# Attention output through DRAM in one transfer, heads laid out by halves of tokens, weight slices used two pieces behind the load

## The chip, the cores and the metric

One core of a Trainium2 chip runs the whole kernel. The metric is the device time of one execution in microseconds (us); the kernel before is given by the median of three runs.

## What is computed

Two blocks over 2048 tokens of width 512, each behind a layer norm whose shift, scale and gate come from a condition vector `c`: multi-query attention (32 heads of width 16, one shared key and value head), and a gated feed-forward part of width 1792 without a nonlinearity.

```python
mod = (_silu(c) @ w_mod).reshape(c.shape[0], 6, 1, -1)        # sa, ca, ga, sb, cb, gb
h = _layernorm(x) * (1 + ca) + sa
q = heads(h @ wq); k = h @ wk; v = h @ wv                     # 32 heads of q, one of k and v
p = softmax(einsum("bhqd,bkd->bhqk", q, k) * 16 ** -0.5)
x = x + ga * (heads_joined(einsum("bhqk,bkd->bhqd", p, v)) @ wo)
h = _layernorm(x) * (1 + cb) + sb
x = x + gb * (((h @ w_gate) * (h @ w_up)) @ w_down)
```

## The kernel before

**Units.** After a lead-in, the kernel runs 32 units, one for every 256 tokens (`ST`) and 128 columns of q (8 heads, one of four chunks `ch`). Within a unit, two heads stand side by side along the 512 columns of a matmul (`BT`): index `a` (0, 1) picks the half of the partitions, index `p` (0, 1) the plane of the tile `sst`, and `c` (0, 1) the half of the 512 columns. Before the change head 4p + 2c + a lies there, and `sst` is laid out as [p, (c, n)].

**Turns and steps.** A unit has 16 turns, one per 128 keys, and a turn has two steps, so 32 steps in a unit (`NSTEP`). In a turn TensorE computes scores of this unit (`qk_exp`, lines 645-657), ScalarE their exponential, TensorE adds probabilities times values of the turn before into one PSUM bank (`pv`, line 664), and TensorE with VectorE find the row maxima of the unit to come (`max_mm`, lines 590-608). Between them stand "side" matmuls (line 508): q projections, output projection and the feed-forward part of earlier tokens. The program order of every engine is written out by `attend` (line 1210) and nothing is reordered later; each engine runs its own list in order and waits only where data or a buffer is missing.

**The result of a unit.** `pv_out` (line 667) stands at the end of turn 1 of the next unit. ScalarE evicts the bank to `ev` (line 670). Ten transfers on the queue of SyncE (SP) follow: two put the sums of the softmax into DRAM (`rs`, line 675), eight lay the eight heads one below the other in the tile `oc` (line 681). `normalise` (line 683) has three parts, placed by `NORM_AT` at steps 5, 12 and 18: `load` brings the sums back spread over 128 partitions (line 688); `recip` inverts them on VectorE (line 691), writes them to DRAM (`ri`, line 693) and at once reads them back repeated for each head's 16 rows (`rr`, line 695); `mult` scales `oc` on GpSimd (POOL, line 700) and makes two halves in 16 bits.

**The side list.** `late_weights` (line 887) returns a list of items, each with a gap in steps to the next; `side_step` (line 1169) takes at most one per step. What an item issues comes at the start of the turn after its step (`posts`, drained at line 1242); the matmuls of the `sums` items are issued at their own step. Three kinds matter here.
- `norms` (line 957): 36 slices of `wo`, `w_gate` and `w_up` are loaded through SP (`stage`, line 925, load at line 931), and one item later squared and added up on POOL (`square`, lines 938 and 940). `sums` (line 942) adds these over the partitions on TensorE (line 950). Gaps: `SQ_GAP`, and `SUM_GAP` once.
- `pipelined` (line 1077): the same slices are loaded again and one item later scaled and split into 16-bit halves on POOL (`split`, lines 1066-1074).
- `row_norms` (line 976): the 14 slices of `w_down` are squared on ScalarE (line 984). Their items stand between those of `pipelined`. The slices of both kinds share six buffers in rotation (`SLOTS`). With two loads per pair of items, the buffer of one row slice is loaded anew by the third next row slice, and `row_norms` squares it four items after its own load: so the square waits for the row slice that was staged one row item before it.

The loads of all slices share the SP queue with `pv_out`, `normalise`, the loads of q (line 563), the row maxima (line 636) and the outputs (line 860).

Of the kernel before, what the change touches and what calls it, by code (L numbers as in the profile page):

```python
# [16 lines left out]
OP = mybir.AluOpType  # L17
# [23 lines left out]
NBANK = 8  # L41
QPRE = 24
Q_LAG = 8
# [19 lines left out]
def adaln_mqa_glu_kernel(ctx: ExitStack, tc: tile.TileContext, x_in, wq_in, wk_in, wv_in, wo_in,  # L63
# [79 lines left out]
    nc.gpsimd.memset(vst, 1.0)  # L143
    sst = []
    for i in range(3):
        t = consts.tile([128, 2, BT], F16, name=f"sst{i}")
        if i == 2:
            nc.gpsimd.memset(t, 0.0)
        sst.append(t)
# [139 lines left out]
        partial(b, [wkv], b)  # L289

    def q_part(u, p):
        partial((u, p), [wqs[u][:, :, 64 * p + 32 * c:64 * p + 32 * c + 32] for c in range(2)], 0)

    def q_evac(u, p):
        split_rows(sst[u][:, p, :], pks[u, p], qsc, sck[:, 3:4], 0.0)
        ps_give(pks[u, p])

    def split_rows(dst, p, scale, mscale, bias):
        hi = work.tile([128, BT], F16, name="hi", tag="x1", bufs=6)
        nc.scalar.activation(hi, p, AF.Identity, bias=bias, scale=mscale)  # L300
        nc.vector.scalar_tensor_tensor(dst, p, scale, hi, op0=OP.mult, op1=OP.subtract)

    def k_evac(b):
# [252 lines left out]
    def load_q(u):  # L556
        sb, ch = divmod(u, NC)
        d = qd[sb // 2, ch].rearrange("(h e) l n -> e h l n", e=16)
        s = sst[u % 3].rearrange("p q (c n) -> p (q c) n", c=2)
# [23 lines left out]

    def max_parts(u):
        if u < NU and u not in mparts:
            mparts[u] = work.tile([128, 2, 2, 4, 4], F32, name="mpart")
            if u == 0:
                nc.vector.memset(mparts[u], LOW)

    def max_mm(u, a, op):  # L590
        kind, p, t, kc = op
        s = sst[u % 3]
        m = ps_sc() if kind == "diff" else ps_mx()
        keys = [kst[:, kc * 512:(kc + 1) * 512]]
        if kind == "diff":
            keys = [kng, kst[:, (kc + 1) * 512:(kc + 2) * 512]]
        for i, w in enumerate(keys):
            nc.tensor.matmul(m, s[64 * a:64 * a + 48, p, t * 128:(t + 1) * 128], w[64 * a:64 * a + 48, :],  # L598
                             start=(i == 0), stop=(i == len(keys) - 1))
        part = mparts[u][:, a, p, t, kc:kc + 1]  # L600
# [15 lines left out]

    def max_fin(u):
        mms[u] = work.tile([128, 2, 8], F32, name="mm")
        nc.vector.tensor_reduce(mms[u], mparts[u].rearrange("p a q t k -> p a (q t) k"), axis=AX.X, op=OP.max)

    def max_rows(u):
        def f():
            mms[u, "b"] = ps_hold("mxt")
            p = mms[u, "b"][0:16, 0:128]
            mms[u, "p"] = p
            nc.tensor.transpose(p, mms[u].rearrange("p a c -> p (a c)"), ident)  # L626

        def g():
            p = mms[u, "p"]
            mt = [work.tile([16, 128], F16, name=f"mt{hl}") for hl in range(2)]  # L630
            nc.scalar.activation(mt[0], p, AF.Copy, scale=1.0 / 32.0)
            nc.vector.scalar_tensor_tensor(mt[1], p, 1.0 / 32.0, mt[0], op0=OP.mult, op1=OP.subtract)
            ps_give(mms[u, "b"])
            s = sst[u % 3]
            for hl in range(2):
                nc.sync.dma_start(s[48 + hl:113 + hl:64, :, :], mt[hl])
        return [(100, f, g)]

    pvb = {}
    ptl = {}  # L640
    oc = {}
    och = {}
    rsum = {}

    def qk_exp(u, kt, p, a, last=False):
        s = sst[u % 3]
        ptl[u, kt, p, a] = work.tile([128, D], F32, name="P", tag="P", bufs=8)
        t = ps_sc()
        cuts = (0, BT // 2, BT) if pending and last else (0, BT)
        for c0, c1 in zip(cuts, cuts[1:]):  # L650
            if c0:
                flush()
            nc.tensor.matmul(t[:, c0:c1], kst[64 * a:64 * a + 50, kt * 128:(kt + 1) * 128],  # L653
                             s[64 * a:64 * a + 50, p, c0:c1], start=True, stop=True)
        ex = nc.scalar.activation(ptl[u, kt, p, a], t, AF.Exp)  # L655
        if sync["due"]:
            sync.update(due=False, exp=ex.ins.name)
# [9 lines left out]
    def pv_out(u):  # L667
        sb, ch = divmod(u, NC)
        ev = work.tile([128, BT], F32, name="ev", tag="ev", bufs=3)
        nc.scalar.activation(ev, pvb[u], AF.Copy, scale=evs)  # L670
        ps_give(pvb[u])
        oc[u] = work.tile([128, ST], F32, name="oc", tag="oc", bufs=2)
        rsum[u] = dram.tile([8, ST], F32, name=f"rs{u}")
        for p in range(2):
            nc.sync.dma_start(rsum[u][4 * p:4 * p + 4, :].rearrange("(c a) n -> a c n", a=2),
                              ev[64 * p + 16:64 * p + 64:32, :].rearrange("a (c n) -> a c n", c=2))
        for c in range(2):
            for j in range(4):
                p, a = divmod(j, 2)
                r = 16 * (4 * p + 2 * c + a)  # L680
                nc.sync.dma_start(oc[u][r:r + 16, :], ev[32 * j:32 * j + 16, c * ST:(c + 1) * ST])  # L681

    def normalise(u):
        st = {}

        def load():
            st["c"] = work.tile([128, 16], F32, name="rc")
            nc.sync.dma_start(st["c"], rsum[u].rearrange("h (p f) -> (h p) f", f=16))

        def recip():  # L690
            nc.vector.reciprocal(st["c"], st["c"])
            st["d"] = dram.tile([8, ST], F32, name=f"ri{u}")
            nc.sync.dma_start(st["d"].rearrange("h (p f) -> (h p) f", f=16), st["c"])
            st["r"] = work.tile([128, ST], F32, name="rr", tag="ev", bufs=3)
            nc.sync.dma_start(st["r"], st["d"][:, None, :].to_broadcast([8, 16, ST]))

        def mult():
            o = oc[u]
# [6 lines left out]
        return load, recip, mult  # L705

    posts = []
    ends = []
# [178 lines left out]
    def late_weights():  # L887
# [69 lines left out]
        def norms(order):  # L957
            ns = [n for m in order for n in range(len(sl)) if sl[n][0] == m]
            out = []
            waiting = deque()  # L960
            for j in range(len(ns) + 1):
                def f(j=j):
                    if j < len(ns):
                        stage(ns[j])
                    if j:
                        square(ns[j - 1])
                out.append((SQ_GAP, nothing, f))
                if waiting and j >= waiting[0][0]:
                    out.append((0,) + sums(*waiting.popleft()[1:]))
                m = sl[ns[j - 1]][0] if j else None  # L970
                if m is not None and (j == len(ns) or sl[ns[j]][0] != m):
                    waiting.extend((j + SUM_LAG, m, n) for n in range(4))
            out.append((SUM_GAP, nothing, nothing))
            return out + [(2,) + sums(*w[1:]) for w in waiting]

# [98 lines left out]
                nc.gpsimd.tensor_tensor(wt[:, 1, i, c], t, wt[:, 0, i, c], op=OP.subtract)  # L1074
            return load, gate, halves

        def pipelined(ns, gap=SPLIT_GAP):
            sp = [split(n) for n in ns]
            out = []
            for n in range(len(ns) + 1):  # L1080
# [17 lines left out]
        return items, pipelined(list(range(n2, len(sl))), LAST_GAP), [m0(k) for k in range(KC)] + [m1, m2, m3]  # L1098

    def run_items(items):  # L1100
        for _, f, post in items:
# [233 lines left out]
    nrm[0]()  # L1335
    cover(3000)
    nrm[1]()
    cover(5000)
    nrm[2]()
    drain_all()  # L1340
    run(wo_work(NS - 1))
    cover(6000)
# [25 lines left out]
```

## Time and profile before

| | |
|---|---|
| median of three runs | 1677.38 us (1677.31 to 1677.66) |
| the profiled execution | 1676.62 us |
| its span, first to last instruction | 1674.8 us |
| TensorE busy | 1647.2 us (98%) |
| VectorE busy | 1403.3 us (84%) |
| ScalarE busy | 1236.2 us (74%) |
| GpSimd (POOL) busy | 525.3 us (31%) |
| mean granted TensorE clock | 0.995 |

In the rows of the trace PE is TensorE's matmuls, PEld its weight loads, DVE is VectorE, ACT is ScalarE, POOL is GpSimd and SPq the queue of SyncE. A timeline row gives start, duration (us), engine, line, operation, tile written and read, and the count; the bracket at its end is the idle time of the engine before it, and what ended it. A row by windows gives, for each stretch, the busy time of every engine with the number of instructions, then the granted TensorE clock, the busy share of the DMA engines and GB/s.

### The profile page before, as it was taken

The numbers are of one execution on the slowest core, as the hardware profiler recorded it, in microseconds if no ns is written. First come the engines' busy times: TensorE is split into PE (matmuls) and PEld (weight loads), VectorE is DVE, ScalarE is ACT, GpSimd is POOL, SyncE is SP. The second block draws the span as 40 slices with busy tenths as digits, with TensorE's granted clock in tenths as the row PEclk, the third lists the DMA queues.
The fourth block names the chain that finished last, engine by engine and source line by source line (L and its number), as shares of the span: only waits on it lengthen the run. The fifth ranks groups of instructions, "written<-read, shape, count | busy, mean of one in ns | idle before, by whom it ended". The sixth has DMA issues, their size and how long they took to land.

```text
span 1674.8 us, 39843 instructions
## 1 busy us (share of the span) xinstructions
PE 1647.2 (98%) x15603; PEld 745.8 (45%) x15603; DVE 1403.3 (84%) x2434; ACT 1236.2 (74%) x2389; POOL 525.3 (31%) x833
## 2 busy tenths in 40 slices
PE   8899899999999999999999999999999999999999
PEld 4333233344533455434544354543545334553776
DVE  7999899987998999999998999999998999870311
ACT  5688788887878777777777777777778777877200
POOL 5766537874671011301122011310122001210322
PEclk9999999999999999999999999999999999999999
DMA  6213213232110000000000000000000000000000
GB/s 241 108 45 94 84 49 107 86 120 85 52 54 19 17 12 26 14 19 20 14 24 7 19 17 25 14 13 19 20 26 7 12 24 25 13 9 14 27 13 13
DMA packets 66024, 67.27 MB, mean 40 GB/s; under 512 B 21542, under 2 KB 50730, under 8 KB 65836
## 3 DMA queue, kind: packets, MB, share of 16 engines
q1 hardware_dynamic: 63724, 64.15, 12.3%
q8 instruction: 122, 2.00, 0.5%
q10 hardware_dynamic: 2112, 0.59, 0.1%
q14 instruction: 66, 0.54, 0.1%
HBM read 51.32 MB, written 8.92 MB: 36 GB/s over the span
## 4 chain that ended last, share of the span: by engine, by line
PE 90%; ACT 3%; DVE 3%; DMA 2%; SPq 1%; issue 1%; POOL 0%; ACTq 0%; DVEq 0%
PE side L508 40%; PE pv L664 29%; PE sc L653 10%; PE mx L598 8%; ACT P L655 2%; DVE mpart L602 1%; SPq L681 1%; DMA xbig<-in_A_x_dram 1%; PE mx L799 1%; DMA kwb<-in_B_w_up_dram 0%; ACT hf L807 0%; DMA kwb<-in_B_w_down_dram 0%; PE mxt L626 0%; PE sc L598 0%; DVE bs L247 0%
## 5 line engine op out<-in xcount | busy, mean ns | idle before, releaser
L602 DVE TENSOR_REDUCE mpart<-mx 128x1 f32<-128x512 f32 x2016 | 1274.9, 684 | 104.9 <-PE mx L598 96.0
L655 ACT ACTIVATE P<-sc 128x512 f32<-128x512 f32 x2048 | 1096.0, 599 | 272.3 <-PE sc L653 218.4
L653 PE MATMUL sc<-sst,kst 50*128 50x512 f16 (+1 forms) x2294 | 695.8, 356 | 0.2
L598 PE MATMUL mx<-kst,sst 48*128 48x512 f16 x2032 | 636.3, 378 | 7.8 <-ACT P L655 5.7
L664 PE MATMUL pv<-P,vst 128*32 128x512 f32 x4096 | 546.9, 606 | 0.9
L508 PE MATMUL side<-h2T,wg 64*128 64x256 f16 (+1 forms) x2368 | 533.4, 271 | 0.5 <-ACT P L655 0.2
L508 PE MATMUL side<-h2T,wu 64*128 64x256 f16 (+1 forms) x2368 | 531.0, 270 | 0.0
L508 PEld LDWEIGHTS <-wg 64*128 64x128 f16 (+1 forms) x2368 | 223.3, 94 | 223.0 <-ACT P L655 188.6
L508 PE MATMUL side<-wd,glu 64*128 64x512 f16 (+1 forms) x1164 | 266.5, 378 | 0.4 <-ACT P L655 0.4
L653 PEld LDWEIGHTS <-kst 50*128 50x128 f16 x2294 | 209.1, 94 | 83.3 <-issue 66.5
L508 PEld LDWEIGHTS <-wu 64*128 64x128 f16 (+1 forms) x2368 | 223.3, 95 | 47.8 <-issue 12.0
L844 POOL TENSOR_SCALAR glu<-gf 128x256 f16<-128x256 f32 x112 | 46.0, 411 | 608.1 <-DVE gf L843 563.4
L598 PEld LDWEIGHTS <-sst 48*128 48x128 f16 x2064 | 190.2, 94 | 33.7 <-issue 15.3
L508 PEld LDWEIGHTS <-glu 64*128 64x128 f16 (+1 forms) x1164 | 97.0, 94 | 194.2 <-ACT P L655 90.2
L664 PEld LDWEIGHTS pv<-P,vst 128*32 128x32 f32 x4096 | 80.8, 108 | 161.9 <-issue 150.7
L843 DVE TENSOR_TENSOR gf<-side,g 128x256 f32<-128x256 f32 x112 | 46.7, 418 | 76.6 <-ACT g L841 64.7
L508 PE MATMUL side<-h,wq 64*128 64x512 f16 (+1 forms) x372 | 96.7, 379 | 0.5 <-ACT P L655 0.4
L841 ACT ACTIVATE g<-side 128x256 f32<-128x256 f32 x112 | 42.3, 379 | 73.0 <-PE side L508 72.6
L700 POOL TENSOR_TENSOR oc<-oc,rr 128x256 f32<-128x256 f32 x31 | 22.6, 730 | 228.3 <-DMA sst<-qd 182.9
L508 PE MATMUL side<-wo,och 64*128 64x512 f16 (+1 forms) x360 | 86.2, 377 | 0.0
L845 POOL TENSOR_TENSOR glu<-gf,glu 128x256 f16<-128x256 f32 x112 | 75.5, 674 | 9.3
L508 PEld LDWEIGHTS <-och 64*128 64x128 f16 (+1 forms) x360 | 30.6, 94 | 66.5 <-ACT P L655 30.2
(231 smaller groups left out, 789.2 us busy)
## 6 DMA issues: line engine op xcount, KB each, us to landing
kwb<-in_B_w_gate_dram SPq DMA_DIRECT2D x32, 224.0 KB
kwb<-in_B_w_up_dram SPq DMA_DIRECT2D x32, 224.0 KB
sst<-qd SPq DMA_DIRECT2D x180, 32.0 KB
qd<-q SPq DMA_DIRECT2D x16, 256.0 KB
oc<-ev SPq DMA_DIRECT2D x256, 16.0 KB
rr<-ri SPq DMA_DIRECT2D x32, 128.0 KB
x<-in_A_x_dram SPq DMA_DIRECT2D x14, 256.0 KB
kwb<-in_B_w_down_dram SPq DMA_DIRECT2D x14, 256.0 KB
```

Source lines behind the costliest of these rows:

```text
L508: return nc.tensor.matmul(self.p[:, c * w:(c + 1) * w], left[rows], right[rows], start=start and c == 0, stop=stop and c == len(terms) - 1)
L598: nc.tensor.matmul(m, s[64 * a:64 * a + 48, p, t * 128:(t + 1) * 128], w[64 * a:64 * a + 48, :], start=(i == 0), stop=(i == len(keys) - 1))
L602: nc.vector.tensor_reduce(part, m, axis=AX.X, op=OP.max)
L653: nc.tensor.matmul(t[:, c0:c1], kst[64 * a:64 * a + 50, kt * 128:(kt + 1) * 128], s[64 * a:64 * a + 50, p, c0:c1], start=True, stop=True)
L655: ex = nc.scalar.activation(ptl[u, kt, p, a], t, AF.Exp)
L664: nc.tensor.matmul(pvb[u][32 * j:32 * j + 32, :], vst[:, kt, :], ptl[u, kt, p, a], start=(kt == 0), stop=(kt == KT - 1))
L681: nc.sync.dma_start(oc[u][r:r + 16, :], ev[32 * j:32 * j + 16, c * ST:(c + 1) * ST])
L700: eng.tensor_tensor(o, o, st["r"], op=OP.mult)
L841: nc.scalar.activation(g, p[:, 0:ST], AF.Copy, scale=2.0 ** -45)
L843: nc.vector.tensor_tensor(gf, p[:, ST:2 * ST], g, op=OP.mult)
L844: nc.gpsimd.tensor_scalar(glu()[:, 0, f, :], gf, 1.0, 0.0, op0=OP.mult, op1=OP.add)
L845: nc.gpsimd.tensor_tensor(glu()[:, 1, f, :], gf, glu()[:, 0, f, :], op=OP.subtract)
```

## The change

- `pv_out` writes the whole evicted tile to DRAM in one transfer (`pd`). `load` (step 5) reads the sums from it, and the heads in two transfers, one for each half of the tokens' columns `c`.
- Head 4c + 2p + a now lies at (c, p, a): `sst` is laid out as [c, p, n], so the moving operand of a score matmul is two runs of 256 columns instead of one of 512, and the order of the row maxima and of the q slices follows.
- `recip` (step 12) ends after the write of the inverses; reading them back is a part of its own, `spread`, at step 15, in two transfers. `mult` goes from step 18 to 19. In the code for the last unit `spread` follows `recip` directly.
- Slices of `norms` and `pipelined` are used two items after their load (`LAG`); the list for `w_down` keeps one. `SQ_GAP` goes from 2.75 to 2.6 and `SUM_GAP` from 5 to 4. `ROW_LAG` and `SLOTS` stay.

```diff
-SQ_GAP = 2.75
+SQ_GAP = 2.6
+LAG = 2
-SUM_GAP = 5.0
+SUM_GAP = 4.0
-NORM_AT = (5, 12, 18)
+NORM_AT = (5, 12, 15, 19)
...
-        t = consts.tile([128, 2, BT], F16, name=f"sst{i}")
+        t = consts.tile([128, 2, 2, ST], F16, name=f"sst{i}")
...
-            nc.tensor.matmul(t[:, c0:c1], kst[64 * a:64 * a + 50, kt * 128:(kt + 1) * 128],
-                             s[64 * a:64 * a + 50, p, c0:c1], start=True, stop=True)
+            nc.tensor.matmul(t.rearrange("k (c n) -> k c n", c=2), keys, s[64 * a:64 * a + 50, :, p, :],
+                             start=True, stop=True)
...
-        oc[u] = work.tile([128, ST], F32, name="oc", tag="oc", bufs=2)
-        rsum[u] = dram.tile([8, ST], F32, name=f"rs{u}")
-        for p in range(2):
-            nc.sync.dma_start(rsum[u][4 * p:4 * p + 4, :].rearrange("(c a) n -> a c n", a=2),
-                              ev[64 * p + 16:64 * p + 64:32, :].rearrange("a (c n) -> a c n", c=2))
-        for c in range(2):
-            for j in range(4):
-                p, a = divmod(j, 2)
-                r = 16 * (4 * p + 2 * c + a)
-                nc.sync.dma_start(oc[u][r:r + 16, :], ev[32 * j:32 * j + 16, c * ST:(c + 1) * ST])
+        pd[u] = dram.tile([128, BT], F32, name=f"pd{u}")
+        nc.sync.dma_start(pd[u], ev)
...
-            nc.sync.dma_start(st["c"], rsum[u].rearrange("h (p f) -> (h p) f", f=16))
+            nc.sync.dma_start(st["c"], pd[u][16:128:32, :].rearrange("j (q f) -> j q f", f=16))
+            oc[u] = work.tile([128, ST], F32, name="oc", tag="oc", bufs=2)
+            heads = pd[u].rearrange("(j r) (c n) -> c j r n", r=32, c=2)
+            for c in range(2):
+                nc.sync.dma_start(oc[u][64 * c:64 * c + 64, :], heads[c, :, 0:16, :])
...
+        def spread():
             st["r"] = work.tile([128, ST], F32, name="rr", tag="ev", bufs=3)
-            nc.sync.dma_start(st["r"], st["d"][:, None, :].to_broadcast([8, 16, ST]))
+            for c in range(2):
+                nc.sync.dma_start(st["r"][64 * c:64 * c + 64, :],
+                                  st["d"][:, None, c * ST:(c + 1) * ST].to_broadcast([4, 16, ST]))
...
-            for j in range(len(ns) + 1):
-                def f(j=j):
+            for j in range(len(ns) + LAG):
+                q = j - LAG
+
+                def f(j=j, q=q):
                     if j < len(ns):
                         stage(ns[j])
-                    if j:
-                        square(ns[j - 1])
+                    if q >= 0:
+                        square(ns[q])
...
-        def pipelined(ns, gap=SPLIT_GAP):
+        def pipelined(ns, gap=SPLIT_GAP, lag=LAG):
...
-                    if n:
-                        sp[n - 1][1]()
-                        sp[n - 1][2]()
+                    if n >= lag:
+                        sp[n - lag][1]()
+                        sp[n - lag][2]()
```

More of the change, by code (lines that the diff above doesn't have):

```diff
@@ L291, in q_part @@
     def q_part(u, p):
-        partial((u, p), [wqs[u][:, :, 64 * p + 32 * c:64 * p + 32 * c + 32] for c in range(2)], 0)
+        partial((u, p), [wqs[u][:, :, 64 * c + 32 * p:64 * c + 32 * p + 32] for c in range(2)], 0)
     def q_evac(u, p):
-        split_rows(sst[u][:, p, :], pks[u, p], qsc, sck[:, 3:4], 0.0)
+        split_rows(sst[u][:, :, p, :], pks[u, p], qsc, sck[:, 3:4], 0.0)
         ps_give(pks[u, p])
@@ L648, in qk_exp @@
         t = ps_sc()
[L649 to L653, printed above, removed]
-                             s[64 * a:64 * a + 50, p, c0:c1], start=True, stop=True)
+        keys = kst[64 * a:64 * a + 50, kt * 128:(kt + 1) * 128]
+        if pending and last:
+            for c in range(2):
+                if c:
+                    flush()
+                nc.tensor.matmul(t[:, c * ST:(c + 1) * ST], keys, s[64 * a:64 * a + 50, c, p, :], start=True, stop=True)
+        else:
+            nc.tensor.matmul(t.rearrange("k (c n) -> k c n", c=2), keys, s[64 * a:64 * a + 50, :, p, :],
+                             start=True, stop=True)
         ex = nc.scalar.activation(ptl[u, kt, p, a], t, AF.Exp)
@@ L704, in mult @@
             och[divmod(u, NC)] = h
-        return load, recip, mult
+        return load, recip, spread, mult
     posts = []
@@ L969, in norms @@
                     out.append((0,) + sums(*waiting.popleft()[1:]))
-                m = sl[ns[j - 1]][0] if j else None
-                if m is not None and (j == len(ns) or sl[ns[j]][0] != m):
-                    waiting.extend((j + SUM_LAG, m, n) for n in range(4))
+                if q >= 0 and (q == len(ns) - 1 or sl[ns[q]][0] != sl[ns[q + 1]][0]):
+                    waiting.extend((j + SUM_LAG, sl[ns[q]][0], n) for n in range(4))
             out.append((SUM_GAP, nothing, nothing))
@@ L1075, in split @@
             return load, gate, halves
-        def pipelined(ns, gap=SPLIT_GAP):
+        def pipelined(ns, gap=SPLIT_GAP, lag=LAG):
             sp = [split(n) for n in ns]
             out = []
-            for n in range(len(ns) + 1):
+            for n in range(len(ns) + lag):
                 def f(n=n):
@@ L1097, in late_weights @@
         items += [(1, nothing, f) for _, _, f in rows_of] + [(1, nothing, last_column), (2, tr, trp), (3, bc, last_scale), (1, nothing, last_inverse)]
-        return items, pipelined(list(range(n2, len(sl))), LAST_GAP), [m0(k) for k in range(KC)] + [m1, m2, m3]
+        return items, pipelined(list(range(n2, len(sl))), LAST_GAP, 1), [m0(k) for k in range(KC)] + [m1, m2, m3]
     def run_items(items):
```

24 lines of the change are left out of this document (14 added, 10 removed).

## The prediction

> **What bounds the kernel now.** I read the page first, for the engine that is busy nearly always, then the waits of that engine, to find what is left.
>
> ```profile
> span 1674.8 us, 39843 instructions
> PE 1647.2 (98%) x15603; PEld 745.8 (45%) x15603; DVE 1403.3 (84%) x2434; ACT 1236.2 (74%) x2389; POOL 525.3 (31%) x833
> ```
> ```profile
> PE mx L598 <- ACT P L655: 5.7, 3, 3.3
> PE mx L950 <- DMA kwb<-in_B_w_up_dram: 4.4, 1, 4.4
> PE sc L598 <- DVE kst L301: 2.1, 1, 2.1
> ```
> TensorE is idle 1674.8 - 1647.2 = 27.6 us, and this is all that the change can give back, besides time at a lower clock. Named waits: 4.4 us for a slice of `w_up`, 5.7 us in three waits for ScalarE, and 2.1 us in the lead-in, which the change doesn't touch. To see where they lie, and what they cost in all, I cut the span into units, from one eviction of line 670 to the next.
>
> ```profile
> 162.24:210.68 48.44, 44.02 (x357) 14.28 (x353) 41.11 (x72) 35.69 (x70) 23.34 (x26) 0.93 0.25 74
> 210.68:253.06 42.38, 41.95 (x357) 13.45 (x353) 42.07 (x77) 35.48 (x71) 15.29 (x17) 1.00 0.15 48
> 253.06:295.27 42.21, 42.11 (x336) 13.38 (x336) 40.90 (x72) 35.02 (x69) 34.18 (x48) 1.00 0.34 107
> ...
> 339.83:387.83 48.00, 45.59 (x491) 23.09 (x487) 42.48 (x73) 40.07 (x86) 33.00 (x48) 1.00 0.43 130
> 387.83:440.57 52.74, 49.21 (x536) 26.38 (x532) 43.55 (x79) 40.49 (x86) 26.71 (x39) 0.97 0.18 54
> 440.57:486.77 46.20, 46.06 (x497) 23.02 (x497) 42.81 (x74) 36.81 (x72) 37.97 (x44) 1.00 0.29 81
> 581.32:627.41 46.09, 46.09 (x533) 25.54 (x529) 42.77 (x74) 36.79 (x72) 7.20 (x13) 1.00 0.05 12
> ```
> The row from 581.32 stands for the later units: TensorE works 46.09 of 46.09 us, SP and POOL have time to spare, and nothing can be won. Three units are longer than their neighbours: unit 2 (row 162.24) by 48.44 - 42.3 = 6.1 us, unit 6 (339.83) by 48.00 - 46.1 = 1.9 us, unit 7 (387.83) by 52.74 - 46.1 = 6.6 us. Two of them have a lowered clock too. The timeline shows what holds TensorE in each.
>
> **Unit 2.**
> ```profile
> 162.98 1.09 SPq L675 DMA_DIRECT2D rs<-ev  x2
> 164.12 5.01 SPq L681 DMA_DIRECT2D oc<-ev  x8
> 169.24 0.52 SPq L931 DMA_DIRECT2D kwb<-in_B_w_up_dram  x1
> ```
> ```profile
> 172.13 0.93 POOL L938 TENSOR_TENSOR kwb<-kwb 128x448 f32<-128x448 f32 x1 [11.00 <-DMA kwb<-in_B_w_up_dram]
> 172.13 0.55 PE L950 MATMUL mx<-kwb,onec 128*32 128x112 f32 x2 [4.42 <-DMA kwb<-in_B_w_up_dram]
> ```
> The ten issues of `pv_out` hold SP for 6.3 us. Behind them stands the load of a slice; POOL waits for it, and the `sums` matmul of line 950 waits for POOL's square, with all of TensorE's list behind it: 4.42 us.
>
> **Unit 7.**
> ```profile
> 388.54 1.10 SPq L675 DMA_DIRECT2D rs<-ev  x2
> 389.69 5.13 SPq L681 DMA_DIRECT2D oc<-ev  x8
> 394.87 0.58 SPq L931 DMA_DIRECT2D kwb<-in_B_w_down_dram  x1
> 395.49 0.44 SPq L688 DMA_DIRECT2D rc<-rs  x1
> ```
> ```profile
> 397.69 0.63 ACT L984 ACTIVATE kwb<-kwb 128x512 f32<-128x512 f32 x1 [3.56 <-DMA kwb<-in_B_w_down_dram]
> 398.95 0.37 PE L598 MATMUL mx<-kst,sst 48*128 48x512 f16 x1 [3.27 <-ACT P L655]
> ```
> The same burst, now ahead of a row slice. ScalarE's square (line 984) waits 3.56 us, the exponentials behind it wait, no bank comes free, TensorE stands for 3.27 us. "ACT P" is only the last link.
>
> **Unit 6.**
> ```profile
> 352.32 0.33 SPq L693 DMA_DIRECT2D ri<-rc  x1
> 357.05 0.67 SPq L695 DMA_DIRECT2D rr<-ri  x1
> ...
> 358.27 0.42 SPq L931 DMA_DIRECT2D kwb<-in_B_w_down_dram  x1
> ```
> ```profile
> 362.18 0.63 ACT L984 ACTIVATE kwb<-kwb 128x512 f32<-128x512 f32 x1 [2.64 <-DMA kwb<-in_B_w_down_dram]
> 363.44 0.37 PE L598 MATMUL mx<-kst,sst 48*128 48x512 f16 x1 [2.20 <-ACT P L655]
> ```
> Here SP waits from 352.65 to 357.05 for `ri` to land before it may issue `rr`, and a row slice comes behind: ScalarE 2.64 us, TensorE 2.20 us.
>
> **What the lowered clock adds.**
> ```profile
> 171.00:177.70 6.70, 5.57 (x26) 1.40 (x28) 2.95 (x5) 2.28 (x4) 5.41 (x6) 0.50 0.31 94
> 357.00:364.00 7.00, 4.80 (x59) 2.70 (x56) 4.78 (x9) 4.36 (x11) 6.58 (x10) 1.00 0.63 187
> 399.70:403.00 3.30, 3.30 (x22) 1.27 (x16) 1.04 (x2) 2.07 (x6) 3.05 (x5) 0.50 0.33 125
> ```
> After the stalls of 4.42 and 3.27 us the granted clock is 0.50, for at least 6.7 and 3.3 us; around the one of 2.20 us it stays 1.00. Work at half clock costs half its time: at most 5.57/2 = 2.8 us, and 3.3/2 = 1.65 us. The Trainium skill (TensorE: Matmul & The Clock Gate, Part 1) says that the clock halves after at least one idle window of about 3.4 us. By that rule the 3.27 us would have halved nothing and unit 7 would give 1.65 us less; this trace shows the halving after 3.27 us, and the trace decides.
>
> **Part by part.**
>
> *One transfer out, three back.* SP's issues in `pv_out` shrink from ten to one: 6.3 us to about 0.55 us (half of the 1.10 for two). So slices staged in turn 2, right behind it, leave 5.8 us earlier. Then `load` at the end of turn 2 must wait until `pd` has landed; that wait is new, and queued behind it on SP are all slices from turn 3 on. The trace shows no write of this size to DRAM that anything waits for. Bounds: the small `ri` write of 182.00 let `rr` go at 183.46, 1.1 us after its issue ended; that of 352.32, behind other transfers, took 4.4 us.
> ```profile
> 182.00 0.33 SPq L693 DMA_DIRECT2D ri<-rc  x1
> 183.46 0.68 SPq L695 DMA_DIRECT2D rr<-ri  x1
> ```
> The nearest row is the slice load of equal size (256 KB): issued at 394.87, used at 397.69, 2.8 us. I take 2.8. The three reads add 0.44 + 2 x 0.68 (the `rr` row: also many rows out of DRAM) = 1.8 us, so SP is through 4.6 us after the eviction, where before it was through `rc` at 395.93 - 388.54 = 7.4 us. Even at 4.7 us from issue to landing it would be 6.5 us, still earlier. The Trainium skill (DMA: Bandwidth & Descriptors, Anatomy of one DMA) puts a fixed cost of about 2.0 us on a DMA, most of it the receipt of the write, heaviest for HBM, plus bytes by 436 GB/s; this speaks against a round trip through DRAM, and gives an estimate of 2.6 us for `pd`, with which SP would be through at 4.4 us.
>
> *`spread` apart from `recip`.* Between them now stand the slices of turn 7, and SP no longer waits there without doing anything; `rr` costs a second issue, 0.68 us. `mult` is half a turn later on POOL; nothing but the output projection reads its result, turns later in every fourth unit: nothing.
>
> *Slices two items behind.* In unit 2 the `sums` matmul at step 7 needs the square of slice 22. Counting the gaps through, that slice is staged at step 2 of unit 2 before (issued in turn 2, behind `pv_out`) and at step 0 after (turn 1, ahead of it). So this stall goes by the order alone, whatever `pd` takes: 6.1 us, the whole excess of unit 2 (4.42 idle and 1.7 of the half clock). The next slices are needed at steps 11 to 19 and staged before step 8: no new wait.
>
> *Row slices keep their order.* Neither `ROW_LAG` nor `SLOTS` changes, and a square still waits for the slice staged one row item before. The list runs one item ahead of before, so the numbers of the slices shift by one, but row items stand at the same steps: again one row load stands behind `pv_out` at turn 2 of unit 7 with its square at turn 4, and one behind the `rr` issues at turn 8 of unit 6 with its square at turn 9. So these two stalls shrink only by what SP is faster.
> - Unit 7: ScalarE asks at 397.69 - 3.56 = 394.13. The load goes at 388.54 + 0.55, or 0.4 later behind the other slice of that turn, and lands 2.8 us later, at about 392.3, by 393.3 if `pd` ahead of it takes a further microsecond. The stall goes: 3.27 + 1.65 = 4.9 us. The next row load goes behind `load`, at about 393.5, lands at 396.3 or a little after, and is asked for one turn later, 394.13 + 46.1/16 = 397.0: in time, or up to 1 us late; I charge 0.3.
> - Unit 6: `ri` again goes at 352.32 (SP waits there for VectorE, whose place is fixed). It landed late because nine transfers held up by the burst had just gone out; those now go 3 to 6 us earlier. At 2 us rather than 4.4, both `rr` are out by 354.7 + 1.4 = 356.1, the row slice lands at about 359, and ScalarE asks at 362.18 - 2.64 = 359.54. The stall goes, barely; of the 1.9 us I count 1.6. If `ri` again takes 4.4 us, all of it stays.
>
> *The two runs of the moving operand.*
> ```profile
> L653 PE MATMUL sc<-sst,kst 50*128 50x512 f16 x1802 | 602.7, 380 | 0.1
> L653 PE MATMUL sc<-sst,kst 50*128 50x256 f16 x492 | 93.1, 268 | 0.1
> ```
> ```profile
> 358.35 0.27 PE L653 MATMUL sc<-sst,kst 50*128 50x256 f16 x1
> ...
> 358.46 0.27 PE L653 MATMUL sc<-sst,kst 50*128 50x256 f16 x1
> ```
> No row has such an operand. As bounds: two separate matmuls of 256 columns start 0.11 us apart, so that even two instructions for the one of 512 take 0.22 us of the array, against its 0.38 us, which includes the fill; one instruction with a break in it should not be dearer. I take 0; with 0.01 us, what the rows resolve, the 1802 would cost up to 18 us. A gain is excluded: the columns are the same.
>
> *Side list.* `SQ_GAP` and `SUM_GAP` bring the list forward by about four steps and the lag gives two or three back; the weights are ready at nearly the same step. The order of row maxima and q loads changes no count. In the tail all the transfers lie under side matmuls, as before.
>
> **Sum.** 6.1 + 1.6 + 4.9 - 0.3 = 12.3 us. The profiled execution took 1676.62 us, 1.8 more than its span, and lies 0.76 below the median of 1677.38; taken from the median this gives 1665.1 us. At the most, with the whole excess of units 2, 6 and 7 (14.6 us), 1662.8.
>
> **Rivals.**
> - *The new wait for DRAM keeps ScalarE waiting.* If `pd` and `ri` take 4.4 us or more, the stall of unit 6 stays (2 us) and the row slice behind `load` in unit 7 is 1.5 to 2 us late. Gain 12.6 - 1.6 - 2 = 9, about 1668.5. For it: the 4.4 us of 352.32. Against it: 1.1 us at 182.33. The rule on the write's receipt in the Trainium skill (DMA: Bandwidth & Descriptors, Anatomy of one DMA) speaks for it too.
> - *The lag binds the SP queue to POOL.* While row slices are loaded too, slice n goes into the buffer of slice n - 3. POOL splits that one in item n - 1 now, and did in item n - 2. So the load comes to wait for the item just before it, with the row slices queued behind it on SP.
> ```profile
> 360.95 0.64 POOL L1072 TENSOR_SCALAR kwb<-kwb,sca 128x448 f32<-128x448 f32 x1
> ...
> 362.33 1.03 POOL L1074 TENSOR_TENSOR wu<-kwb,wu 128x448 f16<-128x448 f32 x1
> ```
> A split takes 2.4 us, a load 2.8, together 5.2, from one item to the square one or two turns after the load; items are 3 steps or 4.3 us apart. If POOL is also held by a feed-forward group, each of 14 squares could wait about 0.5 us: 7 us of the gain gone, 1672. Against it: POOL is free for a third of unit 6.
> - *Slower: the broken operand.* It sits in every unit, on the engine that is the bound. From 12.3/1802 = 7 ns per matmul it eats the gain, from 8.7 ns the kernel is slower by 0.2%; at 15 ns it is 1692. For it: no row shows it free. Against it: the pairs of 256 above.
>
> **Chances.** The forecast (gain of 10 to 14.6 us) 0.62; the wait for DRAM 0.16; the lag 0.09; slower by the operand 0.06; about nothing, with new stalls of this kind elsewhere, 0.07. A difference under 0.2% (3.4 us) can't be told from none. So faster 0.87, same 0.07, slower 0.06. The range is 1661.5, a little past the largest gain, to 1671, which takes in the first rival and most of the second.
>
> **What would show it.** Unit 2 at about 42.4 us without a wait at line 950; unit 7 near 47 to 48 us; unit 6 near 46.5; no granted clock of 0.50 after the lead-in; one issue of `pd` per unit and `rc` some 3 us behind it; score matmuls of 512 columns still at 380 ns; the later units at 46.1 us. I am wrong if those later units lengthen, or if line 984 still ends long idle times of ScalarE.

## The result, and the profile after

The changed kernel took 1667.95 us against 1677.52 us before (medians of four executions each): ratio 0.9937, 95% interval 0.9918 to 0.9957. One of the four changed executions took 4046.45 us, with its matmuls at about twice their time, and is left out of the ratio; the median of the other three is 1667.53 us. Timed again, with five executions, the changed kernel took 1666.66 us against 1677.58 us, ratio 0.9936 (0.9923 to 0.9948). So it is faster by 0.6%, 10 to 11 us, where 12.3 us were forecast. The profile shown here is from the second timing.

That profiled execution took 1665.08 us. The page of the changed kernel:

```profile
span 1662.9 us, 39666 instructions
PE 1642.6 (99%) x15603; PEld 745.1 (45%) x15603; DVE 1401.1 (84%) x2434; ACT 1232.4 (74%) x2389; POOL 523.9 (32%) x833
```
TensorE does the same number of matmuls; its idle time fell from 27.6 to 1662.9 - 1642.6 = 20.3 us. The rest of the 11.9 us of span came out of its busy time: 4.4 us of it in units 2 and 7, whose granted clock was 0.93 and 0.97 before and is 1.00 now.

The units of the changed kernel, by windows (1, 2, 3, 4, 6, 7, 8 and a late one):

```profile
121.81:164.22 42.41, 40.64 (x329) 12.69 (x324) 39.88 (x68) 34.66 (x69) 31.97 (x34) 1.00 0.33 103
164.22:205.44 41.22, 41.22 (x357) 13.98 (x353) 40.87 (x72) 35.48 (x70) 22.58 (x26) 1.00 0.31 93
205.44:249.10 43.66, 42.98 (x364) 14.31 (x361) 43.11 (x80) 35.48 (x71) 17.47 (x24) 1.00 0.15 47
249.10:290.47 41.37, 41.11 (x329) 12.93 (x328) 40.01 (x69) 34.92 (x69) 33.00 (x44) 1.00 0.38 121
335.03:380.51 45.48, 45.27 (x491) 23.10 (x487) 42.39 (x73) 40.59 (x88) 31.03 (x45) 1.00 0.48 143
380.51:429.16 48.65, 47.58 (x536) 25.90 (x532) 43.44 (x79) 39.74 (x84) 26.59 (x39) 1.00 0.17 54
429.16:475.28 46.12, 46.04 (x498) 23.01 (x497) 42.80 (x74) 36.78 (x73) 39.91 (x46) 1.00 0.29 86
569.90:616.01 46.11, 46.11 (x533) 25.54 (x529) 42.80 (x74) 36.81 (x73) 7.14 (x13) 1.00 0.06 18
```
Unit 2 is shorter by 48.44 - 41.22 = 7.2 us, unit 6 by 2.5, unit 7 by 4.1: 13.8 us together. The late units stand still at 46.1. But unit 1, which took 40.4 us before, has 42.41, and TensorE is busy for only 40.64 of them; unit 3 is longer by 1.3 us, and unit 4 shorter by 0.8. Something new costs about 2 us. TensorE's waits name it:

```profile
PE sc L601 <- DVE kst L304: 2.1, 1, 2.1
PE mx L956 <- POOL kwb L946: 1.6, 1, 1.6
```
The timeline of POOL and TensorE at that place:

```profile
122.04 0.62 POOL L546 TENSOR_SCALAR q<-qf 128x512 f16<-128x512 f32 x1 [7.06 <-ACT qf L545]
...
124.86 1.13 POOL L946 TENSOR_TENSOR kwb<-kwb 128x448 f32<-128x448 f32 x1
```
```profile
126.04 0.43 PE L956 MATMUL mx<-kwb,onec 128*32 128x128 f32 x8 [1.59 <-POOL kwb L946]
```
A `sums` matmul of unit 1 stands right behind a square (line 946) that POOL could not begin earlier, because the split of a q projection ahead of it waited for ScalarE. The matmul does need that square: by the code, `wo` and `w_gate` share one tile of sums (`ssqs[0]`, chosen by `m % 3 != 0`). The last `sums` matmul of `wo` reads columns 384 to 511 of it, and the square in front of it, that of slice 9, adds a piece of `w_gate` to columns 448 to 895. (The squares of `wo` have by then been overwritten by those of `w_gate`; both kernels leave them out.) With the lag of one the same square stands a turn earlier, ahead of that split: it is done at 118.35, and its matmul runs at 122.28 without a wait. This is the kind of stall that the change was to remove, at another place.

The SP queue at the start of unit 7, where the burst stood:

```profile
381.22 0.33 SPq L679 DMA_DIRECT2D pd<-ev  x1
381.60 0.42 SPq L937 DMA_DIRECT2D kwb<-in_B_w_down_dram  x1
383.57 0.58 SPq L686 DMA_DIRECT2D rc<-pd  x1
384.20 1.09 SPq L690 DMA_DIRECT2D oc<-pd  x2
...
385.84 0.43 SPq L937 DMA_DIRECT2D kwb<-in_B_w_down_dram  x1
```
```profile
390.03 0.63 ACT L991 ACTIVATE kwb<-kwb 128x512 f32<-128x512 f32 x1 [0.64 <-DMA kwb<-in_B_w_down_dram]
```
The row slice that was held up for 6.3 us now goes 0.38 us after `pd`. SP then waits for `pd` to land, 2.35 us after its issue, and is through at 385.29, 4.1 us after the eviction (4.6 forecast). The one row square that still waits, 0.64 us, is that of the slice behind `load`.

### The profile page after: what moved, and what is told of

It is laid out like the page before. It is cut to its first block, busy times and chain, and to the rows that moved or that the text cites. A ratio compares the mean times of both kernels' runs of the same rounds, so it can differ in the third digit from the quotient of the medians.

```text
span 4044.3 us, 39666 instructions
## 1 busy us (share of the span) xinstructions
PE 4037.2 (100%) x15603; PEld 1229.1 (30%) x15603; DVE 1471.8 (36%) x2434; ACT 1345.2 (33%) x2389; POOL 521.1 (13%) x833
## 4 chain that ended last, share of the span: by engine, by line
PE 100%; DVE 0%; DMA 0%; issue 0%
PE side L511 37%; PE pv L670 30%; PE mx L601 15%; PE sc L659 13%; PE sc L657 2%; PE misc L169 1%; PE pk L287 0%; PE part L279 0%; PE mx L805 0%; PE sc L267 0%; PE sc L601 0%; PE misc L901 0%; PE pvt L317 0%; PE mxt L629 0%; PE mx L956 0%; PE misc L339 0%
## 5 line engine op out<-in xcount | busy, mean ns | idle before, releaser
L601 PE MATMUL mx<-kst,sst 48*128 48x512 f16 x2032 | 1435.3, 819 | 0.0
L659 PE MATMUL sc<-sst,kst 50*128 50x512 f16 x1802 | 1287.0, 784 | 0.0
L670 PE MATMUL pv<-P,vst 128*32 128x512 f32 x4096 | 1258.8, 1326 | 0.0
L511 PE MATMUL side<-h2T,wu 64*128 64x256 f16 (+1 forms) x2368 | 1239.5, 532 | 0.0
L511 PE MATMUL side<-h2T,wg 64*128 64x256 f16 (+1 forms) x2368 | 1201.4, 517 | 0.0
L511 PE MATMUL side<-wd,glu 64*128 64x512 f16 (+1 forms) x1164 | 679.3, 814 | 0.0
L511 PEld LDWEIGHTS <-wg 64*128 64x128 f16 (+1 forms) x2368 | 382.3, 162 | 745.0 <-issue 474.1
L511 PEld LDWEIGHTS <-wu 64*128 64x128 f16 (+1 forms) x2368 | 392.5, 166 | 155.7 <-issue 2.0
L511 PE MATMUL side<-h,wq 64*128 64x512 f16 (+1 forms) x372 | 242.8, 828 | 0.0
L657 PE MATMUL sc<-sst,kst 50*128 50x256 f16 x492 | 206.1, 534 | 0.0
```

The lines of the kernel that those rows point to most:

```text
L511: return nc.tensor.matmul(self.p[:, c * w:(c + 1) * w], left[rows], right[rows], start=start and c == 0, stop=stop and c == len(terms) - 1)
L601: nc.tensor.matmul(m, s[64 * a:64 * a + 48, t // 2, p, t % 2 * 128:(t % 2 + 1) * 128], w[64 * a:64 * a + 48, :], start=(i == 0), stop=(i = ...
L657: nc.tensor.matmul(t[:, c * ST:(c + 1) * ST], keys, s[64 * a:64 * a + 50, c, p, :], start=True, stop=True)
L659: nc.tensor.matmul(t.rearrange("k (c n) -> k c n", c=2), keys, s[64 * a:64 * a + 50, :, p, :], start=True, stop=True)
L670: nc.tensor.matmul(pvb[u][32 * j:32 * j + 32, :], vst[:, kt, :], ptl[u, kt, p, a], start=(kt == 0), stop=(kt == KT - 1))
```

## Experiments

All medians are in us. The kernel before, timed beside them, had 1677.58 in the first four, 1677.17 in the next four, 1678.33 in the next three and 1677.39 in the last.

| kernel | median | ratio to before (95%) |
|---|---|---|
| changed kernel | 1666.66 | 0.9936 (0.9923 to 0.9948) |
| lag and gaps alone | 1676.56 | 0.9993 (0.9984 to 1.0002) |
| changed, lag of one | 1666.97 | 0.9936 (0.9922 to 0.9949) |
| head layout alone | 1676.69 | 0.9997 (0.9988 to 1.0006) |
| lag in the splitting only | 1666.84 | 0.9935 (0.9923 to 0.9947) |
| `spread` joined to `recip` | 1669.84 | 0.9956 (0.9944 to 0.9967) |
| `pd` written in eight | 1674.62 | 0.9977 (0.9968 to 0.9987) |
| `spread` alone | 1676.71 | 0.9997 (0.9988 to 1.0006) |
| before with `ROW_LAG` 2 | 1671.47 | 0.9966 (0.9954 to 0.9979) |
| lag in the splitting, `ROW_LAG` 2 | 1663.03 | 0.9912 (0.9898 to 0.9927) |
| lag in the splitting, `spread` at 17 | 1664.58 | 0.9924 (0.9911 to 0.9937) |
| lag of one, `ROW_LAG` 2 | 1661.64 | 0.9910 (0.9894 to 0.9927) |

### The changed kernel again

> The changed kernel once more, for an undisturbed profile and a closer time. Theory (three stalls behind the SP queue are gone): 1665 to 1668 us; unit 2 about 42.4 us with no wait at the sums matmul, unit 7 at 47 to 48 us, unit 6 near 46.5 us, no granted clock of 0.50 after the lead-in. Rival (the wait for DRAM keeps ScalarE waiting): unit 6 still at 48 us and a wait of 1 to 2 us in unit 7 behind the reads of pd; that would be the 2 to 3 us by which the first timing (1667.9) lies above the forecast of 1665.1. Rival (the broken operand costs): the later units above 46.1 us by 0.1 us or more each, which over 24 units would be the same 2 to 3 us.

Measured: 1666.66 us. The forecast's places hold (41.22, 45.48 and 48.65 us in units 2, 6 and 7; no half clock after the lead-in in this profile). Neither rival explains what is missing to 1665.1: the late units did not lengthen, and unit 6 is short. In this profile it is the stall of unit 1.

### Lag and gaps alone

```diff
-SQ_GAP = 2.75
+SQ_GAP = 2.6
+LAG = 2
-SUM_GAP = 5.0
+SUM_GAP = 4.0
...
-            for j in range(len(ns) + 1):
+            for j in range(len(ns) + LAG):
...
-        def pipelined(ns, gap=SPLIT_GAP):
+        def pipelined(ns, gap=SPLIT_GAP, lag=LAG):
```

> The kernel before with only the lag of two and the shorter gaps; the ten transfers and the read right behind the write of the inverses stay. Theory: the stall of unit 2 goes by the order alone, those of units 6 and 7 stay: 1677.4 - 6.1 = 1671.4 us. Rival (the lag binds the SP queue to POOL): row squares wait more often, and units 6 and 7 together get longer by 2 to 7 us: 1673 to 1678 us.

Measured: 1676.56 us, hardly a gain, and 5 us above the theory. Unit 2 went to 41.22 us, as the theory said. But in the profile, which is of the longest of the eleven executions (1678.02 us), unit 1 took 43.89 us, with the stall seen above, and units 6 and 7 took 51.87 and 54.30 us, longer than before. The list now runs one item ahead, so a row square of unit 6 comes earlier and meets the slices held up by the burst: TensorE stands for 3.70 us there instead of 2.20. The total agrees with the rival; its mechanism (POOL holding SP) is not what the timeline shows: the slices left SP one right behind the other once the burst was through. POOL may still have a part in it: by the profile ScalarE's wait of 4.15 us ended with POOL's split of an `up` slice, which had itself waited 1.03 us for that slice.

### The changed kernel with a lag of one

```diff
-SQ_GAP = 2.6
-LAG = 2
+SQ_GAP = 2.75
+LAG = 1
-SUM_GAP = 4.0
+SUM_GAP = 5.0
```

> The changed kernel with the lag of one and the gaps of before: the transfer to DRAM, the reads back, the separate spread and the head layout stay. Theory: SP is through with the eviction 5.8 us earlier, so the slice of unit 2, which POOL missed by about as much as the 4.4 us stall, lands in time without the lag; gain as in the full change within 1 to 2 us, 1665 to 1669 us. If only the lag can remove the stall of unit 2: 1671 to 1674 us. Rival (the lag costs): faster than the full change by more than 1 us.

Measured: 1666.97 us, the same as the full change. Unit 2 took 41.21 us without any lag, unit 1 40.40 us, and unit 6 46.40 us with a stall of 0.84 us. The lag wins 0.9 us in unit 6 and 0.2 in unit 7, and loses 2.0 in unit 1 and 0.4 in units 3 and 4. (That the two profiles have the same span, 1662.9 us, is chance: with the lag of one the first eviction comes 0.9 us later, behind a spell of half clock in the lead-in that the other profile has not.) All the gain of the change is in the transfers and the separate `spread`.

### Head layout alone

```diff
-                             s[64 * a:64 * a + 50, p, c0:c1], start=True, stop=True)
+            nc.tensor.matmul(t.rearrange("k (c n) -> k c n", c=2), keys, s[64 * a:64 * a + 50, :, p, :],
+                             start=True, stop=True)
```
The slices of `wq`, the order of the maxima and the eight targets in `oc` follow; the ten transfers stay.

> The kernel before with only the head layout by halves of tokens, so that the score matmul streams two runs of 256 columns; ten transfers, lag and gaps as before. Theory: the operand costs nothing, 1677.4 us within 1 us, score matmuls at 380 ns. Rival (the broken operand costs): 2 us or more above, and the later units above 46.1 us each.

Measured: 1676.69 us, no difference. The groups by form of this kernel, with the moving operand in two runs:

```profile
L659 PE MATMUL sc<-sst,kst 50*128 50x512 f16 x1802 | 602.6, 380 | 0.1
L657 PE MATMUL sc<-sst,kst 50*128 50x256 f16 x492 | 93.3, 269 | 0.1
```
380 ns, as with one run of 512. The rival that would have made the kernel slower shows no price. Unit 6 took 46.74 us in this profile, with a stall of 1.19 us rather than 2.20, with the ten transfers as before.

### The lag in the splitting only

```diff
-SQ_GAP = 2.6
+SQ_GAP = 2.75
-SUM_GAP = 4.0
+SUM_GAP = 5.0
...
-            for j in range(len(ns) + LAG):
-                q = j - LAG
+            for j in range(len(ns) + 1):
+                q = j - 1
```

> The changed kernel with the lag of two in the splitting only; the squares ahead of the sums keep the lag of one and the gaps of before. Theory: the lag of the squares puts one sums matmul of unit 1 (step 5) right behind a square that POOL has not done yet, 1.6 us of stall and in some executions a spell of half clock; without it unit 1 is back at 40.4 us (from 42.4), units 3 and 4 together at 84.6 (from 85.0), and unit 6 keeps 45.5: about 2.4 us faster than the changed kernel, 1664 to 1665 us. Rival (the stall of unit 1 is time that the next units win back, or the lag of the squares is needed in unit 2): 1666 to 1668 us.

Measured: 1666.84 us, a miss in the total. Unit 1 is back at 40.39 us and units 3 and 4 at 42.37 and 42.24, as expected. But unit 6 took 49.00 us. The SP queue and ScalarE at that place:

```profile
345.18 0.33 SPq L695 DMA_DIRECT2D ri<-rc  x1
345.60 0.38 SPq L937 DMA_DIRECT2D kwb<-in_B_w_up_dram  x1
348.76 1.10 SPq L700 DMA_DIRECT2D rr<-ri  x2
349.92 0.45 SPq L937 DMA_DIRECT2D kwb<-in_B_w_down_dram  x1
```
```profile
354.48 0.63 ACT L991 ACTIVATE kwb<-kwb 128x512 f32<-128x512 f32 x1 [2.45 <-DMA kwb<-in_B_w_down_dram]
```
The same in the changed kernel:

```profile
347.52 0.33 SPq L695 DMA_DIRECT2D ri<-rc  x1
347.95 0.38 SPq L937 DMA_DIRECT2D kwb<-in_B_w_up_dram  x1
350.39 1.09 SPq L700 DMA_DIRECT2D rr<-ri  x2
351.53 0.45 SPq L937 DMA_DIRECT2D kwb<-in_B_w_down_dram  x1
```
```profile
354.86 0.63 ACT L991 ACTIVATE kwb<-kwb 128x512 f32<-128x512 f32 x1 [0.49 <-POOL wu L1080]
```
The order is the same, and in both ScalarE asks for the slice 6.85 us after `ri` went (352.03 and 354.37). In the one `rr` goes 3.58 us after `ri` and the slice lands within 4.6 us; in the other 2.87 and 3.3 us. Between these two profiles the landing times make the difference. The six executions of this kernel lie in two groups, 1663.44 to 1665.47 us and 1668.20 to 1668.98 us, but this stall alone does not tell them apart: the profiled execution has it, and it is the one of 1665.47 us. What the other three have besides is not shown.

### `spread` joined to `recip`, and `spread` alone

```diff
-NORM_AT = (5, 12, 15, 19)
+NORM_AT = (5, 12, 19)
...
-        def spread():
```

> The changed kernel with the read of the inverses right behind their write again (two transfers, no slices between). Theory: with the burst gone the write of the inverses lands in 2 to 2.5 us, so SP is held about that long at step 12 and one slice of turn 7 goes 2 us later; the row square of unit 6 waits 0 to 1 us: 1666 to 1668 us. Rival (the separate spread is what removed the stall of unit 6): unit 6 again at 47.5 to 48 us, 1668.5 to 1670 us with a spell of half clock.

Measured: 1669.84 us, 3.2 us more than the changed kernel (the two intervals overlap a little), and unit 6 at 47.41 us, 1.9 more: the rival is right, but for the half clock, which did not follow there. `ri` took until 351.90 to let `rr` go, 3 us after its issue at 348.90, the row square waited 2.42 us and TensorE 1.86. Not all of the 3.2 us need be the part's: in this profile unit 1 took 43.93 us, at half clock behind the same stall as in the changed kernel, and unit 7 took 49.57 us, because `pd` let its read go only after 3.90 us there. The other way round, the kernel before with only this part:

```diff
-NORM_AT = (5, 12, 18)
+NORM_AT = (5, 12, 15, 19)
...
+        def spread():
             st["r"] = work.tile([128, ST], F32, name="rr", tag="ev", bufs=3)
```

> The kernel before with only the read of the inverses moved to step 15 and the product to step 19; the ten transfers stay. Theory: in unit 6 the row slice still stands behind a late write of the inverses, so that stall keeps 1.5 to 2.2 us, and units 2 and 7 are untouched: 1676 to 1677.6 us. Rival (the separate spread is worth something by itself): unit 6 at 46 us, 1675 us or less.

Measured: 1676.71 us. The total stayed, as the theory had it, but unit 6 went to 46.25 us, with a stall of 0.71 us, which is the rival's number. Unit 7 of that profile took 54.01 us rather than 52.74, and the median can't tell 1.7 us from the variation of the executions. Nor does one profile price the part: the kernel with the head layout alone, which reads the inverses back at once, had 46.74 us in unit 6.

### `pd` written in eight

```diff
-        nc.sync.dma_start(pd[u], ev)
+        for r in range(0, 128, 16):
+            nc.sync.dma_start(pd[u][r:r + 16, :], ev[r:r + 16, :])
```
The lag is one, the gaps are those of before.

> The route through DRAM, lag of one, gaps of before, and the result written in eight transfers of 16 rows rather than one. Theory (SP's time in issuing is the cost, not the route): eight issues of 0.4 to 0.6 us hold SP for 3 to 5 us, a good part of the stalls of units 2 and 7 comes back: 1670 to 1675 us. Rival (it was the transfers between SBUF tiles, or their packets, that delayed the slices): the time stays at that of the one transfer with the same lag, 1667 us.

Measured: 1674.62 us, 7.7 us above the same kernel with one transfer (6.9 by the two ratios). The route is the same, only the number of issues differs. SP and TensorE of this kernel at the places of the two old stalls:

```profile
164.70 3.58 SPq L680 DMA_DIRECT2D pd<-ev  x8
...
382.68 5.23 SPq L680 DMA_DIRECT2D pd<-ev  x8
```
```profile
171.15 0.35 PE L957 MATMUL mx<-kwb,onec 128*32 128x112 f32 x2 [1.72 <-DMA kwb<-in_B_w_up_dram]
...
392.00 0.37 PE L601 MATMUL mx<-kst,sst 48*128 48x512 f16 x1 [2.18 <-ACT P L661]
```
Both stalls are back, with a second one of 2.41 us in unit 7 and one of 1.62 us in unit 1, where a load of q came late; the units 1, 2 and 7 take 42.10, 43.28 and 55.23 us. The second one of unit 7 is the next row square, which waited 2.86 us: `load` could go only at 389.30, when the eight writes had landed, and the row slice behind it left SP at 391.62. SP's time in issuing is the cost.

### `ROW_LAG` 2, in the kernel before and in two versions of the change

```diff
-ROW_LAG = 4
+ROW_LAG = 2
```

> The kernel before with one digit changed, ROW_LAG 2 for 4: a row slice is squared before its buffer is loaded anew, so that the square waits for a slice staged two row items earlier and no longer for that of one item earlier. (The computation changes in this: every row slice of w_down is now squared itself, where before the first three were overwritten first.) Theory (the stalls of units 6 and 7 are row squares that wait for a load just issued behind the burst or the inverses): both go, unit 6 at 46 us and unit 7 at 47 to 48 us with all ten transfers in place, unit 2 stays at 48.4: 1677.3 - 6.5 = 1670.8 us. Rival (the SP queue is late as a whole, whichever slice is waited for): within 2 us of the kernel before.

Measured: 1671.47 us, 6.9 us less than before with all ten transfers in place (5.7 by the ratio); 6.5 were expected. Unit 7 took 48.23 us, 4.5 less. Unit 6 took 47.76 us, not 46: with the squares two items earlier one of them now stands right behind the burst and waits 1.95 us. So that the total came out is in part luck: unit 6 gave 0.2 us for the 2 expected, and unit 2, of which nothing was expected, gave 1.0 with a shorter spell of half clock. In unit 7 the late slice was late for the row square alone. With `ROW_LAG` 4 the square finds in its buffer the slice of three row items later, so the kernels with 4 leave the first three slices of `w_down` out of their norms, and those with 2 do not.

> The changed kernel with the lag of two in the splitting only, gaps of before, and ROW_LAG 2. Theory: no stall of unit 1 (as with the lag in the splitting only), and no row square that depends on whether the write of the inverses lands in 2.5 or 3.3 us: unit 6 at 45.5 us in every execution, 1663.5 to 1665 us, and the executions lie closer together than 1663.4 to 1669.0. Rival (the spread of the executions comes from elsewhere, as the phase of the clock's windows in the lead-in): median again 1666 to 1667 us with the same spread.

Measured: 1663.03 us, in five executions from 1661.93 to 1663.56. Unit 1 took 40.40, unit 2 41.22, unit 6 45.29 and unit 7 47.82 us. The spread came out as the theory said, 1.6 us against 5.5; the median lies 0.5 us below its range.

```diff
-NORM_AT = (5, 12, 15, 19)
+NORM_AT = (5, 12, 17, 21)
```
(on the kernel with the lag in the splitting only, `ROW_LAG` 4)

> As the kernel with the lag in the splitting only, but the read of the inverses at step 17 and the product at step 21, so that the row slice of turn 8 goes ahead of it on SP; ROW_LAG stays 4. Theory: the stall of unit 6 (1.9 us and a spell of half clock in the last profile) goes in the same way: 1664 to 1665 us. Rival (another slice stands behind the read then, and is late in its place): 1666 to 1668 us.

Measured: 1664.58 us. Unit 6 took 45.29 us; the stall there is gone by order alone. A wait of TensorE of 1.53 us stayed in unit 7. SP and ScalarE there:

```profile
378.54 0.33 SPq L679 DMA_DIRECT2D pd<-ev  x1
...
382.38 0.58 SPq L686 DMA_DIRECT2D rc<-pd  x1
...
384.67 0.43 SPq L937 DMA_DIRECT2D kwb<-in_B_w_down_dram  x1
```
```profile
388.81 0.63 ACT L991 ACTIVATE kwb<-kwb 128x512 f32<-128x512 f32 x1 [2.09 <-DMA kwb<-in_B_w_down_dram]
```
Here `pd` let its read go only 3.84 us after its issue, where it was 2.35 in the changed kernel, and the row square behind `load` waited 2.09 us for 0.64. This is the first rival of the prediction, in its part for unit 7.

> The transfer through DRAM, the separate spread and the head layout, with ROW_LAG 2, the lag of one everywhere and the gaps of before: the last kernel but one without any lag of two. Theory (the lag of two adds nothing once the burst is gone and the row squares wait for an older slice): 1662 to 1664 us, unit 2 at 41.2 and unit 6 at 45.3 to 45.6 us. Rival (the lag in the splitting keeps POOL and SP apart in units 5 to 7): stalls of about 1 us come back in unit 6, 1664.5 us or more.

Measured: 1661.64 us (1661.47 to 1662.89), the fastest of all: transfers, `spread` and layout of the change, one digit in `ROW_LAG`, and no lag of two at all. Units 1, 2, 6 and 7 took 40.39, 41.22, 45.29 and 47.25 us, and TensorE waited nowhere longer than 0.42 us after the lead-in, although `pd` again took 3.81 us in unit 7: the row squares no longer wait for the slice behind it. The median lies 0.4 us below the range of the theory. Against the changed kernel (0.9936, 0.9923 to 0.9948) its ratio of 0.9910 (0.9894 to 0.9927) is lower by 0.26%, 4 to 5 us; the two intervals overlap a little.

## Why the prediction was right, and where not

- **The bound and the places** were right: the late units did not move, and 13.8 us came out of units 2, 6 and 7, where 12.6 us were forecast (6.1, 1.6 and 4.9; measured 7.2, 2.5 and 4.1). Unit 2 gave more than its whole excess because the 42.3 us taken as normal were its neighbours'; without a stall it takes 41.2. Unit 7 gave 0.8 less: TensorE waits 0.78 us there at 410.76 for VectorE, whose list had just waited 1.45 us for POOL with the last scale.
- **The reading of unit 2** had one link wrong. The `sums` matmul does not wait for POOL's square. Both started at 172.13, released by the same load, and of the eight matmuls only the last two waited (the kernel before):
```profile
167.34 0.37 PE L950 MATMUL mx<-kwb,onec 128*32 128x112 f32 x6
172.13 0.55 PE L950 MATMUL mx<-kwb,onec 128*32 128x112 f32 x2 [4.42 <-DMA kwb<-in_B_w_up_dram]
```
  By the code, two of the six buffers of `SLOTS` lie in the tile of sums `ssqs[0]`, number 6 wholly and number 7 in part. Slice 22 is loaded into buffer 6, and the last two matmuls read columns there. So they wait for the load itself, and what they add up there is the loaded slice and not squares, in both kernels. The slice and its place in the list were right, so the forecast did not suffer.
- **The cause**, SP held by ten issues, is shown by `pd` written in eight: the same route, and 7.7 us lost.
- **"This stall goes by the order alone"** holds for unit 2 (the lag alone: 41.22 us), but the transfers alone remove it too (41.21 us). So I gave 6.1 us to the lag that the other part would have won without it.
- **"No new wait"** is the step that failed. I followed the `sums` matmuls of unit 2 through the list and not those of unit 1. There the lag puts the square that one of them needs a turn later, behind POOL's split of a q projection, and the matmul right behind it at step 5; that costs 2.0 us in unit 1, and 0.4 us in units 3 and 4 together. With the lag out of the squares unit 1 was back at 40.39 us. This is what the sum lacked: 13.8 - 2.4 = 11.4 us of the 11.5 between the two profiled executions. That this lies so near the forecast of 12.3 is in part luck, since the three places gave 1.5 us more than the sum had.
- **The new wait for DRAM** was cheap in the profile of the changed kernel: 2.0 to 2.4 us for `pd` in units 1 to 8, against 2.8 taken. But it varies in unit 7: 2.2 to 2.4 us in three profiles with one `pd`, 3.8 to 4.3 in four others. With 3.90 and 3.84 us (`spread` joined, and `spread` at 17) TensorE stood for 0.91 and 1.53 us behind the row square; with `ROW_LAG` 2 nothing waited. So the first rival's wait exists, and that it is missing in the changed kernel's profile is in part luck. The Trainium skill (DMA: Bandwidth & Descriptors, Anatomy of one DMA) gives its fit for transfers issued by GpSimd, and the estimate from it was 2.6 us; these were issued by SP, and the rows lie on both sides of it.
- **"The stall goes, barely"** in unit 6 was right by a small margin: `rr` could go 2.87 us after `ri` in one profile and 3.58 in another, and with 3.58 the stall is there. The separate `spread`, to which I gave little, is worth 1.9 us there in the changed kernel (47.41 against 45.48).
- **The operand** in two runs costs nothing measurable, as taken.

Left open: what decides how long `pd` and `ri` take to land, what the longer three executions of the kernel with the lag in the splitting have besides the stall of unit 6, and whether POOL has a part in the stall of unit 6 with the lag alone.

## What to carry to other kernels

An engine's queue that only issues transfers is a resource with an order of its own: ten small issues or one wait for a landing hold everything behind them, and the damage appears on an engine that has nothing to do with them. Ask of each late load which instruction reads it first and how many items lie between: here one digit (`ROW_LAG`, how many items a row slice is left lying) was worth more than the lag that was added elsewhere, and moving a list by one item removed one stall and made another. When a margin is a few tenths of a microsecond, executions can fall on both sides of it; here a wider margin showed as a narrower spread as well as in the median.

## What was not expected of the hardware

**The half clock does not follow from the length of the gap alone.** The stall of 1.59 us in unit 1 stands in the changed kernel and in the one with the lag alone. The same stretch behind it, by windows, first in the changed kernel, then with the lag alone:

```profile
125.90:129.20 3.30, 3.15 (x32) 1.17 (x34) 2.63 (x5) 2.07 (x4) 3.14 (x5) 1.00 0.60 176
```
```profile
125.90:129.20 3.30, 3.30 (x24) 0.96 (x22) 2.25 (x4) 1.83 (x4) 1.82 (x2) 0.50 0.12 32
```
Granted clock 1.00 in one and 0.50 in the other after the same gap (unit 1: 42.41 and 43.89 us), while the gaps of 2.20 us before the change and of 2.18 us with `pd` in eight were followed by 1.00. The Trainium skill (TensorE: Matmul & The Clock Gate, Part 1) speaks of an idle window of about 3.4 us that runs freely; by that length neither would have halved the clock, and here 1.59 us sufficed in one execution. So the price of the same stall differed by 1.5 us between these two executions.

**The issue of a transfer is not priced by its size.** The instructions of one line, as shortest/median/longest in ns, of `pd` in the changed kernel (256 KB, 128 partitions) and of `oc` in the kernel before (16 KB, 16 partitions):

```profile
L679 SPq DMA_DIRECT2D pd<-ev x32: 319/340/382, 122.6 to 1544.0; - x32
```
```profile
L681 SPq DMA_DIRECT2D oc<-ev x256: 574/587/1555, 123.7 to 1561.5; - x128
```
By the medians the large one holds SP for 0.34 us, the small one for 0.59 us.
